# A fused attention and MLP kernel: the order of a key, two openings, one product and one mask on VectorE and ScalarE

## The chip, the cores and the metric

The kernel runs on one core of one Trainium2 chip. A core has five engines that run side by side, each through its own instructions in the order in which they were written: TensorE (PE in the profile; its weight loads, PEld, are listed apart), VectorE (DVE), ScalarE (ACT), GpSimd (POOL) and SyncE (SP). They wait for each other on semaphores. SP, ACT and POOL also issue DMAs. The metric is the time of one execution in device microseconds, as the median of several runs. All times below are microseconds.

## What is computed

Two stages follow each other. The first is a decaying linear attention over 4 batches, 8 heads, 768 positions and 64 channels, in blocks of 64 positions; the second is an MLP with a Mish activation over the 3072 tokens that come out.

```python
for b in range(nb):                      # attention, block after block
    intra = einsum('bhic,bhjc->bhij', qb, kb) * Dmask     # lam ** (i - j), i >= j
    intra = einsum('bhij,bhjd->bhid', intra, vb)
    inter = einsum('bhid,bhde->bhie', qb * lam_pow, kv_state)
    out[:, :, sl] = intra + inter
    kv_state = lam_block * kv_state + einsum('bhsd,bhse->bhde', kb * rev_pow, vb)
x = out.transpose(0, 2, 1, 3).reshape(3072, 512)
h = x @ w_in                                              # 512 -> 2048
g = h * tanh(log(1 + exp(h)))                             # Mish
out = g @ w_out                                           # 2048 -> 512
```

## The kernel before

**Tiling.** The kernel uses blocks of 128 positions, so there are 6 groups n = 0 to 5, each with one block of all 4 batches: 512 tokens. Block i = 4n + b is that of group n and batch b. While the MLP of group n runs, the attention of group n + 1 runs between its products, and the loads of group n + 2 are issued. The order on every engine is the order of the Python calls: nothing reorders it.

**The MLP as Strassen-like products.** In groups 1 to 5 both matrix products are made from quarters with seven instead of eight products, called P1 to P7. For the first MLP product the 16 blocks of hidden units are split into four sets of four: set 0 is called A, set 1 B, set 2 C; in groups 2 to 4 the fourth set is made by plain products, `duo(g, half)`: eight 128x256 products into a PSUM bank of the pair "ph", then a Mish on ScalarE (line 463). `set_unit(n, g, step)` (line 535) makes one step of a set: P1 to P7 are four products each at line 599. Around them stand

- `open` (line 576): a ScalarE copy of u1, which P1 left in SBUF, into the PSUM bank of z. P6, P7 and P4 then add to z.
- P5 leaves p5 (called p in the trace; for C in groups 2 to 4 by VectorE into "side", line 609, otherwise by ScalarE, line 611), and `mid` adds p5 to z on VectorE into y (line 561). P7 adds p5 to z into a buffer (hs or side, line 561), and its Mish is `m7`; `late` is the Mish of y; P4 ends with a Mish of z (line 557).
- `x_sum` (line 523): four token sums of x on VectorE, which P5, P6, P7 and P3 read.

The z of A lies in the only bank of "pS", that of B in the only bank of "pk". The score products of the pair at unit 2 use pS for their first tile, pk for their second and the two banks of "po" for the other two. So A's opening waits until the first mask has read its scores, and B's until the second has.

The second MLP product is `fast_unit(n, step, blk)`: eight 128x256 products a call at line 657. Its token sums `token_sum(n, i, part)` run on VectorE (line 640): gsum(i) has two halves, part 0 and 1, and P5, P6, P7 and P3 read gsum 0, 1, 2 and 3. In group 1 the z of this product lies in pk and is opened by a ScalarE copy (line 700) which is put off: it runs inside the next pair of scores, from the list `between`.

**The attention between them.** `scale_k(i)` is the key: one VectorE instruction that scales block i's k with its decay (ktil, line 265). `turn(i)` makes the key if it is not there yet and issues two DMA transposes from SP, of q and of the key (qraw and kraw, line 275). `pair_a` multiplies key and v of two blocks (pv, line 329) and adds the old state in four VectorE instructions (raw, line 289). `pair_s` makes the scores of two blocks (pS, line 352) and the state's part of the output (pO, line 360), then four VectorE masks (sb, line 368); whatever is in `between` runs after the first mask. `pair_o` adds masks times v to pO (line 381) and scales the result (xtok, line 389), which SP transposes into the x of the next group (xt, line 393).

**The order.** For each group a list `units` holds the MLP's steps, and dictionaries say what else is called behind unit u: `sums` (token sums), `ks` (keys), `turns`, `visit` (the pairs), `slots` (loads on POOL, each behind a small POOL copy, line 407, that waits for the latest Mish). Behind a unit the calls come in this order: loads, token sums, keys, turns, the pair, and at last x_sum. In groups 2 to 4, `pair_a` of the group's own blocks 2 and 3 stands at unit 0; `pair_s` of the next group's blocks 0 and 1 at unit 2 and its `pair_o` at unit 13; `pair_s` of the next group's blocks 2 and 3 at unit 17 and its `pair_o` at unit 21. The keys of the change are those of these last two blocks, so their transposes are read at unit 17. x_sum stands behind unit 2. Groups 1 and 5 have lists of their own.

Of the kernel before, what the change touches and what calls it, by code (L numbers as in the profile page):

```python
# [20 lines left out]
def kernel(  # L21
# [11 lines left out]
    B, H, S, D = q.shape  # L33
# [305 lines left out]
    between = []  # L339
# [285 lines left out]
    def token_sum(n, i, part):  # L625

        if (n, i) not in gsum:
            gsum[n, i] = work.tile([128, HK, 2 * C], F16, name=f"gsum{i}", tag=f"gsum{i}", bufs=1)
        w = HK // 2
        ks = slice(part * w, part * w + w)  # L630
        kh = slice(HK + part * w, HK + part * w + w)
        h = hsg[n]
        lo, hi = slice(0, 2 * C), slice(2 * C, 4 * C)
        a, b, op = (
            lambda: (h[:, ks, hi], h[:, kh, hi], ALU.add),
            lambda: (gsum[n, 0][:, ks, :], h[:, ks, lo], ALU.subtract),
            lambda: (h[:, ks, lo], h[:, ks, hi], ALU.subtract),
            lambda: (h[:, kh, lo], gsum[n, 1][:, ks, :], ALU.subtract),
        )[i]()
        nc.vector.tensor_tensor(out=gsum[n, i][:, ks, :], in0=a, in1=b, op=op)  # L640
# [191 lines left out]
    sums = {3: ((2, 0),), 7: ((2, 1),), 11: ((0, 0), (1, 0), (3, 0)), 15: ((0, 1), (1, 1)), 21: ((3, 1),)}  # L832
# [36 lines left out]
    for n in range(1, NG):  # L869
        r, s, t = Pair(), Pair(), Pair()  # L870
        r.n, r.bs, s.n, s.bs, t.n, t.bs = n, (2, 3), n + 1, (0, 1), n + 1, (2, 3)
        def duo(g, half):
            return mm1_duo, (n, g, half * (GT // 2), (half + 1) * (GT // 2))

        def part(g, *steps):
            return [(set_unit, (n, g, step)) for step in steps]

        later = []
        if n < NG - 2:
            later += [lambda f=f, i=(n + 2) * B + b + c: f(i)  # L880
                      for b in (0, 2) for f in (load_k, load_q) for c in range(2)]
        if 1 < n < NG - 1:
            for at, b in zip((2, 3, 6, 7), range(B)):
                later.insert(at, lambda i=(n + 1) * B + b: load_v(i))
        if n == 1:
            units = [[duo(0, 0)], [duo(1, 0)], [duo(2, 0)], part(0, "P1") + part(1, "P1") + [duo(3, 0)],
                     part(0, "P2") + part(1, "P2") + [duo(0, 1)]]
            units += [part(0, "open") + [duo(1, 1)], part(1, "open") + [(mm1_duo, (n, 2, GT // 2, GT, True))],
                      part(0, "P5") + [(duo_mish, (n, 2, 1))] + part(1, "P5"), part(0, "P6", "mid") + part(1, "P6"),
                      [duo(3, 1)] + part(1, "mid"), part(0, "P7") + part(1, "P7"), part(0, "P3") + part(1, "P3"),  # L890
                      part(0, "P4") + part(1, "P4") + part(0, "late") + part(1, "late")]
        else:
            units = [part(2, "P1") + part(0, "P1") + part(1, "P1"), part(2, "P2") + part(0, "P2") + part(1, "P2"),
                     [duo(2, 0)], [duo(3, 0)], part(0, "open") + [duo(2, 1)], [duo(3, 1)],
                     part(0, "P5") + part(2, "P5", "open"), part(0, "P6", "mid") + part(1, "open", "P5"),
                     part(2, "P6", "mid") + part(1, "P6", "mid"), part(0, "P3", "late", "P7"),
                     part(2, "P3", "late") + part(0, "m7") + part(2, "P7"),
                     part(1, "P3") + part(2, "m7") + part(1, "P7", "m7"),
                     part(2, "P4") + part(0, "P4") + part(1, "P4", "late")]
        sums = {12: ((0, 0), (0, 1), (1, 0), (1, 1)), 15: ((2, 0), (2, 1)), 18: ((3, 0),), 19: ((3, 1),)}  # L900
        visit = {}
        if n == 1:
            sums[9], sums[15], sums[19] = ((2, 0),), ((2, 1),), ((3, 0), (3, 1))
            sums[12] = (0, 0), (0, 1), (1, 0)
            del sums[18]
            visit = {10: (pair_a, s), 14: (pair_s, s), 18: (pair_o, s), 21: (pair_s, t), 24: (pair_o, t)}
            ks = {1: 9, 2: 10, 5: 11, 19: 12, 22: 13}
            turns = {1: 9, 5: 10, 7: 11, 19: 12, 22: 13}
            slots = range(6, 14)
        else:  # L910
            if n < NG - 1:
                visit = {0: (pair_a, r), 2: (pair_s, s), 13: (pair_o, s), 17: (pair_s, t), 21: (pair_o, t)}
            if n < NG - 2:
                visit[24] = pair_a, s
            ks = {1: (n + 1) * B + 2, 2: (n + 1) * B + 3, 11: (n + 2) * B, 11.5: (n + 2) * B + 1}
            turns = dict(zip((5, 6, 14, 15), ks.values()))
            slots = (1, 2, 3, 4, 5, 6, 7, 8, 9, 10, 12, 13)
        if n == NG - 1:
            K, L, A, B_ = 2, 3, 0, 1
            units = [part(K, "P1") + part(L, "P1") + part(A, "P1") + part(B_, "P1"),  # L920
                     part(K, "P2") + part(L, "P2") + part(A, "P2") + part(B_, "P2"),
                     part(K, "P5") + part(L, "P5") + part(A, "P5") + part(B_, "P5"),
                     part(K, "P6", "mid") + part(L, "P6", "mid") + part(A, "P6", "mid") + part(B_, "P6", "mid"),
                     part(K, "P3", "late") + part(L, "P3", "late") + part(K, "P7") + part(L, "P7"),
                     part(A, "P3", "late") + part(B_, "P3", "late") + part(A, "P7") + part(B_, "P7"),
                     part(K, "P4") + part(L, "P4") + part(A, "P4") + part(B_, "P4")]
            sums = {8: ((0, 0), (0, 1), (1, 0), (1, 1)), 10: ((2, 0), (2, 1)), 13: ((3, 0), (3, 1))}
        steps = ("P1", "P5", "P6", "P2", "P7", "P3", "P4")
        if n == NG - 1:
            steps = ("P1", "P2", "P5", "P6", "P7", "P3", "P4")  # L930
        units += [[(fast_unit, (n, step, blk))] for step in steps for blk in range(2)]
        for u, calls in enumerate(units):
            for fn, args in calls:
                fn(*args, **({"then": opened} if n == 1 and args[1:] == ("P1", 1) else {}))
            if n == 1 and u == 0:
                turn(8)
                look_s(7)
            if n == 1 and u == 2:
                f = look_kv(7)
                look_o(7)  # L940
                f()
                next_state(1, 1)
            for _ in range({0: 1, 1: 1, 2: 2, 3: 2}.get(u, 0) if n == 1 else 0):
                pace()
                ahead.pop(0)()
            if later and u in slots:
                pace()
                later.pop(0)()
            for i, part in sums.get(u, ()):
                token_sum(n, i, part)  # L950
            if 1 < n < NG - 1 and u == 11:
                next_state(n, 1)
            if n == NG - 2 and u in (22, 24):
                if u == 22:
                    more_sums()
                for i in range(2):
                    in_sum(3, u - 22 + i)
            for at in (u, u + 0.5):
                if ks.get(at, NG * B) < NG * B:
                    scale_k(ks[at])  # L960
            if turns.get(u, NG * B) < NG * B:
                turn(turns[u])
            if n == 1 and u == 7:
                for i in range(4):
                    in_sum(2, i)
            if u in visit:
                f, s_ = visit[u]
                s_.spare = ("pO", "pq") if n == 1 else ("po", "po") if u < 13 else ("pS", "pk")
                s_.scores = [(g, 2 if g in ("po", "ph") else 1) for g in (
                    ("pk", "pS", "ph", "ph") if n == 1 and u < 15 else ("pS", "ph", "po", "po") if n == 1 else  # L970
                    ("pS", "pk", "po", "po") if u < 13 else ("pS", "pk", "ph", "ph"))]
                if n == 1 and u == 14:
                    between += [opened.pop(), lambda: token_sum(1, 1, 1)]
                f(s_)
            if n == 1 and u == 10:
                next_state(2, 0)
            if u == (26 if n == 1 else 25):
                while owed:
                    owed.pop(0)()
            if u == (3 if n == 1 else 2 if n < NG - 1 else 0):  # L980
                for i in range(0, 4):
                    x_sum(n, i)
# [30 lines left out]
```

## Time and profile before

| | us |
|---|---|
| median of 3 runs | 197.01 |
| lowest and highest run | 196.90, 197.21 |
| the profiled execution | 196.51 |
| its span, first to last instruction | 194.7 |
| TensorE busy | 186.6 |
| VectorE busy | 166.4 |
| ScalarE busy | 104.0 |
| GpSimd busy | 80.9 |

The granted TensorE clock is 1.00 over the span. Group 1 is worked on from about 50 to 80 us, groups 2, 3 and 4 from 80.4, 109.4 and 138.3, group 5 from 167 on.

How to read the rows: a row of the timeline has the start, the length from the first start to the last end, the engine, the line, the operation, out<-in, the shape and the count of the instructions that it merges. A bracket tells how long the engine was idle before the row, and what ended that. The ends of matmuls are modelled, the starts are not; consecutive instructions of an engine overlap a little, so the step from one start to the next is shorter than an instruction. "issue" as the end of a wait means that the profile shows no single cause. A row of the waits has the total, the number and the longest. A row of the chain has start, length, engine, tile and line.

### The profile page before, as it was taken

What the parts mean: (1) busy time and instruction counts of PE and PEld (TensorE: products, weight loads), DVE (VectorE), ACT (ScalarE), POOL (GpSimd) and SP (SyncE); (2) the same over time, 40 slices, a digit from 0 to 9 for tenths busy, and PEclk for the clock granted to TensorE, in tenths of its full rate; (3) what the DMA queues carried; (4) which work ended last, traced back from release to release, by engine and by line L of the source; (5) the groups of instructions that cost most, each with busy time, mean ns of one, the idle gap of its engine ahead of it and who ended that gap; (6) DMA issues with size and microseconds to landing.
All of it is one profiled execution on the core that took longest, in us unless ns stands there. A gap on an engine that the chain in (4) does not pass through costs nothing.

```text
span 194.7 us, 5075 instructions
## 1 busy us (share of the span) xinstructions
PE 186.6 (96%) x2021; PEld 154.6 (79%) x2021; DVE 166.4 (85%) x325; ACT 104.0 (53%) x192; POOL 80.9 (42%) x129
## 2 busy tenths in 40 slices
PE   7888999899999999999999999999999999999993
PEld 3554447788888888988889988889988889888882
DVE  7889689699997999799999799998899799555893
ACT  5794674242687631477831477831578821688300
POOL 7997333489397850049730069630063000000000
PEclk9999999999999999999999999999999999999999
DMA  8999999999999998469999889999599023600014
GB/s 131 142 151 191 207 205 205 159 167 202 214 112 160 167 139 138 83 166 159 148 136 176 131 207 159 155 117 161 109 205 152 5 54 84 189 3 0 14 43 162
DMA packets 112458, 26.82 MB, mean 138 GB/s; under 512 B 101554, under 2 KB 112434, under 8 KB 112434
## 3 DMA queue, kind: packets, MB, share of 16 engines
q0 software_dynamic: 77552, 13.37, 95.9%
q1 hardware_dynamic: 31664, 10.76, 30.7%
q10 hardware_dynamic: 3218, 2.36, 4.0%
q8 instruction: 16, 0.26, 0.5%
q14 instruction: 8, 0.07, 0.2%
HBM read 27.26 MB, written 6.29 MB: 172 GB/s over the span
## 4 chain that ended last, share of the span: by engine, by line
PE 65%; DVE 13%; DMA 10%; POOL 8%; issue 2%; ACT 1%; POOLq 0%; DVEq 0%; ACTq 0%
PE z L657 13%; DMA wout<-in_moe_w_out_dram 10%; PE sz L599 9%; PE x L657 7%; PE y L657 5%; PE sx L599 5%; PE ph L451 4%; PE w L657 4%; DVE sb L368 3%; PE sw L599 3%; PE sy L599 3%; DVE raw L289 2%; PE pO L381 2%; POOL win L93 2%; POOL vz L78 2%
## 5 line engine op out<-in xcount | busy, mean ns | idle before, releaser
L657 PEld LDWEIGHTS <-gsum 128*128 128x128 f16 x384 | 36.6, 98 | 5.6 <-issue 1.1
L407 POOL COPY paced<-hsg 1x1 f16<-1x1 f16 x42 | 12.0, 285 | 48.3 <-ACT hsg L557 44.6
L657 PEld LDWEIGHTS <-hsg 128*128 128x128 f16 x272 | 26.1, 98 | 3.2
L75 POOL DMA_DIRECT2D qn<-in_q_dram x23 | 20.4, 886 | 7.0 <-DMA wout<-in_moe_w_out_dram 4.3
L657 PE MATMUL z<-tsum,gsum 128*128 128x256 f16 x176 | 22.5, 273 | 0.7 <-DVE tsum L483 0.6
L67 POOL DMA_DIRECT2D kn<-in_k_dram x23 | 20.5, 893 | 6.4 <-DMA win<-in_moe_w_in_dram 2.3
L78 POOL DMA_DIRECT2D vz<-in_v_dram x24 | 21.1, 884 | 4.0 <-DMA wout<-in_moe_w_out_dram 1.7
L657 PE MATMUL x<-wout,hsg 128*128 128x256 f16 x176 | 21.7, 273 | 0.0
L368 DVE TENSOR_TENSOR sb<-pS,maskT 128x512 f16<-128x512 f32 x32 | 20.0, 684 | 0.3 <-PE pS L352 0.2
L640 DVE TENSOR_TENSOR gsum<-hsg 128x1024 f16<-128x1024 f16 x24 | 15.7, 687 | 5.0 <-ACT hsg L557 3.4
L451 PE MATMUL ph<-xt,win 128*128 128x256 f16 x160 | 19.3, 273 | 0.0
L599 PEld LDWEIGHTS <-win 128*128 128x128 f16 x180 | 17.4, 98 | 1.9
L599 PEld LDWEIGHTS <-isum 128*128 128x128 f16 x160 | 15.6, 97 | 2.8 <-issue 0.8
L451 PEld LDWEIGHTS <-win 128*128 128x128 f16 x160 | 15.3, 98 | 2.0
L463 ACT ACTIVATE hsg<-ph 128x512 f16<-128x512 f32 x20 | 11.9, 595 | 6.4 <-PE ph L451 5.7
L416 PE MATMUL ph<-xt,win 128*128 128x512 f16 x64 | 14.5, 379 | 0.3 <-ACT xt L257 0.3
L265 DVE TENSOR_TENSOR ktil<-kn,lk 128x512 f16<-128x512 f16 (+1 forms) x22 | 14.5, 687 | 0.1
L599 PE MATMUL sx<-xt,win 128*128 128x256 f16 x120 | 14.6, 273 | 0.0
L719 ACT ACTIVATE osum<-z 128x512 f32<-128x512 f32 x4 | 2.4, 597 | 22.2 <-PE z L657 22.2
L561 DVE TENSOR_TENSOR sy<-sz,p 128x512 f32<-128x512 f32 x12 | 8.0, 693 | 5.6 <-PE sz L599 5.4
L428 ACT ACTIVATE hsg<-ph 128x512 f16<-128x512 f32 x16 | 9.6, 597 | 5.8 <-PE ph L416 5.8
L289 DVE TENSOR_TENSOR raw<-pv,state 64x256 f32<-64x256 f32 x24 | 10.1, 420 | 2.8 <-PE pv L329 2.4
(141 smaller groups left out, 378.0 us busy)
## 6 DMA issues: line engine op xcount, KB each, us to landing
out_dram<-osum SPq DMA_DIRECT2D x15, 256.0 KB, 2.7
vz<-in_v_dram POOLq DMA_DIRECT2D x24, 128.0 KB, 5.6
kn<-in_k_dram POOLq DMA_DIRECT2D x23, 128.0 KB, 5.6
qn<-in_q_dram POOLq DMA_DIRECT2D x23, 128.0 KB, 6.0
wout<-in_moe_w_out_dram POOLq DMA_DIRECT2D x4, 512.0 KB, 16.5
out_dram<-osum ACTq DMA_DIRECT2D x8, 256.0 KB, 3.2
win<-in_moe_w_in_dram POOLq DMA_DIRECT2D x3, 512.0 KB, 10.1
win<-in_moe_w_in_dram POOLq DMA_DIRECT2D x2, 256.0 KB, 6.2
```

The lines of the kernel that those rows point to most:

```text
L67: nc.gpsimd.dma_start(out=kn[i], in_=chunk_rows(k, i))
L75: nc.gpsimd.dma_start(out=qn[i], in_=chunk_rows(q, i))
L78: nc.gpsimd.dma_start(out=vz[i % NVB][:, :, 0:D], in_=chunk_rows(v, i))
L265: (nc.gpsimd if B + 1 < i < 2 * B else nc.vector).tensor_tensor(out=t, in0=kn[i], in1=bc(lk, 2, D), op=ALU.mult)
L289: nc.vector.tensor_tensor(out=raw[rs, b % 2, j0 : j0 + nj, :], in0=pv[rs, :, rs], in1=olds(rs), op=ALU.add)
L368: nc.vector.tensor_tensor(out=s.sb[m][t], in0=sc[m][t], in1=bc(maskT, 1, JP), op=ALU.mult)
L407: nc.gpsimd.tensor_copy(paced, mark[-1])
L416: nc.tensor.matmul(ph_t[ni][:, lo:hi], w_in(ni, kc), xt[n][:, kc, lo:hi], start=(kc == 0), stop=(kc == NKC - 1),)
L451: nc.tensor.matmul(t[:, m, lo - half * h : hi - half * h], w_in(ni, kc), xt[n][:, kc, lo:hi], start=(m == 0 and kc == 0), stop=(kc == NKC ...
L599: nc.tensor.matmul(t[:, m, :], lhs(kk, m), rhs(kk), start=(step in ("P1", "P5") and m == 0 and kk == 0), stop=(kk == KH - 1), skip_group_c ...
L640: nc.vector.tensor_tensor(out=gsum[n, i][:, ks, :], in0=a, in1=b, op=op)
L657: nc.tensor.matmul(places(n, key)[:, blk, lo:hi], lhs(kk, blk), rhs(kk, lo, hi), start=(fresh and kk == 0 and blk == 0), stop=(kk == HK - ...
```

## The change

Five edits of the order; no instruction is added, removed or changed.

- In groups 2 to 4 the keys that stood behind units 1 and 2 (both before the masks of unit 2, both after the raw rows of unit 0) now stand behind units 0 and 1; the one behind unit 0 comes ahead of the raw rows of the pair there. The `turns` read the same values in the same order and stay at units 5, 6, 14 and 15. `ks` had its entries at 1 and 2 by name: its first at unit 1, its second at unit 2.
- A's opening moves from unit 4 to unit 3, ahead of that unit's plain products and Mish.
- B's opening moves from unit 7, between A's P6 and B's P5, to unit 4, ahead of that unit's plain products and Mish.
- In unit 12 A's P4 comes first, then C's, then B's; it was C, A, B.
- In group 1 the first half of gsum(1) leaves unit 12, where it came ahead of the masks of unit 14, and goes into `between`, behind the first of these masks and the put-off opening, ahead of the second half.

```diff
-                     [duo(2, 0)], [duo(3, 0)], part(0, "open") + [duo(2, 1)], [duo(3, 1)],
-                     part(0, "P5") + part(2, "P5", "open"), part(0, "P6", "mid") + part(1, "open", "P5"),
+                     [duo(2, 0)], part(0, "open") + [duo(3, 0)], part(1, "open") + [duo(2, 1)], [duo(3, 1)],
+                     part(0, "P5") + part(2, "P5", "open"), part(0, "P6", "mid") + part(1, "P5"),
...
-                     part(2, "P4") + part(0, "P4") + part(1, "P4", "late")]
+                     part(0, "P4") + part(2, "P4") + part(1, "P4", "late")]
...
-            sums[12] = (0, 0), (0, 1), (1, 0)
+            sums[12] = (0, 0), (0, 1)
...
-            ks = {1: (n + 1) * B + 2, 2: (n + 1) * B + 3, 11: (n + 2) * B, 11.5: (n + 2) * B + 1}
+            ks = {0: (n + 1) * B + 2, 1: (n + 1) * B + 3, 11: (n + 2) * B, 11.5: (n + 2) * B + 1}
...
-                    between += [opened.pop(), lambda: token_sum(1, 1, 1)]
+                    between += [opened.pop()] + [lambda p=p: token_sum(1, 1, p) for p in range(2)]
```

## The prediction

> **What bounds the kernel now.** First the page, its engine table and its chain of work.
>
> ```profile
> PE 186.6 (96%) x2021; PEld 154.6 (79%) x2021; DVE 166.4 (85%) x325; ACT 104.0 (53%) x192; POOL 80.9 (42%) x129
> ...
> PE 65%; DVE 13%; DMA 10%; POOL 8%; issue 2%; ACT 1%; POOLq 0%; DVEq 0%; ACTq 0%
> ```
>
> TensorE is busy for 96% of the span and carries 65% of the chain. No part of the change adds or removes an instruction, so it can win only what TensorE idles, and lose only by new idle time. The weight loads show that idle time, since their ends are not modelled. Second view: the waits of the weight loads from 55 to 180 us.
>
> ```profile
> PEld L352 <- issue: 1.7, 8, 0.2
> PEld L599 <- issue: 0.8, 3, 0.3
> PEld L657 <- issue: 0.3, 1, 0.3
> ```
>
> The eight gaps ahead of line 352 are alike (0.21 each) and lie at the first score product of every pair; nothing in the change touches them. The other four are the prize: three at line 599, one per group 2, 3 and 4, and one at line 657 in group 1. Third view, the chain in order of time, at the start of group 3: what ends the wait at line 599.
>
> ```profile
> 114.83 1.88 DVE sb L368 x3
> 116.71 0.34 DVE xsum L523
> 117.09 1.03 PE sw L599 x8
> ```
>
> VectorE ends it: masks (sb), then the first token sum of x (xsum), then P5 of A (sw).
>
> **The change part by part.** *Group 1, the mask ahead of a token sum.* The timeline of all engines:
>
> ```profile
> 66.54 1.29 DVE L640 TENSOR_TENSOR gsum<-hsg 128x1024 f16<-128x1024 f16 x2
> ...
> 67.75 0.68 DVE L640 TENSOR_TENSOR gsum<-gsum,hsg 128x1024 f16<-128x1024 f16 x1
> 67.85 1.75 PEld L657 LDWEIGHTS <-gsum 128*128 128x128 f16 x17
> ...
> 68.46 0.69 DVE L368 TENSOR_TENSOR sb<-pS,maskT 128x512 f16<-128x512 f32 x1
> 69.07 0.68 DVE L640 TENSOR_TENSOR gsum<-gsum,hsg 128x1024 f16<-128x1024 f16 x1
> 69.25 0.58 ACT L700 ACTIVATE z<-x 128x512 f32<-128x512 f32 x1 [2.20 <-DVE sb L368]
> ...
> 69.67 1.88 DVE L368 TENSOR_TENSOR sb<-pS,maskT 128x512 f16<-128x512 f32 x3
> ...
> 69.88 1.62 PEld L657 LDWEIGHTS <-gsum 128*128 128x128 f16 x15 [0.28 <-issue]
> ```
>
> P6 (from 69.88) waits 0.28 for ScalarE's copy z, and that waits for the first mask at 68.46. The change moves the token sum of 67.75 behind this mask. The mask then starts at the end of the two sums (66.54 + 1.29 = 67.83, and 0.03 as between 68.43 and 68.46), 67.86; the copy follows 0.79 later as now (69.25 - 68.46), 68.65, and ends at 69.23. P5's sixteen products end at 69.60, so the wait goes whole, with 0.37 to spare. What is late next? The moved sum runs 68.46 to 69.14, ahead of P6; the other sum keeps 69.07 to 69.75, and P6 needs it from its fifth product, 69.60 + 4 x 0.109 = 70.04. The three later masks stay at 69.67 to 71.55; the products that read the last one (pO, after P6) would want it 0.28 earlier, at 71.68. All fit. Gain 0.28.
>
> *Groups 2 to 4, one key at unit 0.* In group 3, engine by engine:
>
> ```profile
> 111.12 1.74 DVE L289 TENSOR_TENSOR raw<-pv,state 64x256 f32<-64x256 f32 x4 [0.66 <-PE pv L329]
> 112.90 1.29 DVE L265 TENSOR_TENSOR ktil<-kn,lk 128x512 f16<-128x512 f16 x2
> 114.22 2.48 DVE L368 TENSOR_TENSOR sb<-pS,maskT 128x512 f16<-128x512 f32 x4
> 116.62 0.42 DVE L523 TENSOR_TENSOR xsum<-xt 128x512 f16<-128x512 f16 x1
> ```
>
> ```profile
> 113.42 0.65 PE L352 MATMUL pS<-qraw,kraw 64*128 64x128 f16 x16
> ...
> 114.23 2.79 PE L451 MATMUL ph<-xt,win 128*128 128x256 f16 x24
> ```
>
> ```profile
> 117.09 0.31 PEld L599 LDWEIGHTS <-isum 128*128 128x128 f16 x3 [0.24 <-issue]
> ...
> 118.73 0.45 PEld L599 LDWEIGHTS <-w 128*128 128x128 f16 x4
> 119.19 0.51 PEld L599 LDWEIGHTS <-isum 128*128 128x128 f16 x4
> ...
> 121.89 0.42 PEld L599 LDWEIGHTS <-isum 128*128 128x128 f16 x4
> 122.33 0.49 PEld L599 LDWEIGHTS <-w 128*128 128x128 f16 x4
> ```
>
> Between the state rows and the masks stand two keys (1.29), now both behind the raw rows. One of them goes ahead of the raw rows, into VectorE's wait for their products: 0.66 here. VectorE's waits for these products, summed:
>
> ```profile
> DVE raw L289 <- PE pv L329: 2.4, 3, 1.1
> ```
>
> So 1.1 in one group (group 2) and 0.66 in the two others. A key takes the engine for about 0.60 (1.29 for two, the second ending 0.69 after its start), so the wait hides it; without that cover it would cost its 0.60 again. The remaining key then ends at 112.90 + 0.69 = 113.59. The mask cannot start before its scores: its own eight of the sixteen products of 113.42 are through halfway, near 113.83; all sixteen end at 114.07. I take 113.86, since the first mask of this pair reads the first eight, and keep 114.07 as the worse end. Masks and x sum move up by 0.36 (at worst 0.15): xsum from 116.62 to 116.26, and with the 0.47 that P5 now starts behind it (117.09 - 116.62), P5 could start at 116.73. TensorE is through with its 24 products at 114.23 + 24 x 0.109 = 116.85. The 0.24 goes whole, 0.12 to spare. No DMA is moved: the transposes of these keys keep their units, and the loads that SP and POOL issue keep their order.
>
> *The openings of A and B.* Each is a ScalarE copy of u1 into z. ScalarE in group 3:
>
> ```profile
> 115.32 0.60 ACT L463 ACTIVATE hsg<-ph 128x512 f16<-128x512 f32 x1 [1.20 <-PE ph L451]
> ...
> 116.33 1.33 ACT L463 ACTIVATE hsg<-ph 128x512 f16<-128x512 f32 x2
> 117.72 0.60 ACT L611 ACTIVATE p<-sw 128x512 f32<-128x512 f32 x1
> 118.22 0.60 ACT L576 ACTIVATE sz<-side 128x512 f32<-128x512 f32 x1
> 118.74 0.59 ACT L576 ACTIVATE sz<-u 128x512 f32<-128x512 f32 x1
> ```
>
> B's opening (118.74) ends at 119.33, and B's P6 starts late: four loads take 0.51 where the others take 0.42 to 0.43, a loss of 0.08. Moved to unit 4 it takes the place that A's has now, between the Mish of 115.32 and that of 116.33. A's moves ahead of the Mish of 115.32, into a wait of 1.20. It has to wait for the first mask, whose bank it fills, and all later Mish stand behind it: mask at 113.86, opening at 114.65 (the 0.79 of above), next instruction 0.52 later (118.22 to 118.74), 115.17, ahead of 115.32. It is hidden; with the mask at 114.07 the Mish would begin 0.06 late. What is late next is ScalarE itself. The second Mish of the row at 116.33 starts at 117.06 (it ends at 117.66) and waits for TensorE, which does not move there; A's copy p can start 0.49 behind it, 117.55, though P5 is 0.24 earlier. Then C's opening starts at 118.05, ends at 118.65, and C's P6 starts near 118.69 rather than at the 118.61 that TensorE could. So 0.06 more is lost there than now (0.45 against 0.43 at 118.73).
>
> *P4 of A first.* C's P4 loses 0.07 now (0.49 against 0.42 at 122.33), since it waits for VectorE's sum.
>
> ```profile
> 121.76 0.69 DVE L561 TENSOR_TENSOR side<-sz,side 128x512 f32<-128x512 f32 x1 [0.18 <-PE sz L599]
> 122.64 0.69 DVE L561 TENSOR_TENSOR hs<-sz,p 128x512 f32<-128x512 f32 x1 [0.18 <-PE sz L599]
> ```
>
> The first row is C's sum, the second B's. With A first, C's P4 is ready in time; B's is still third. B's sum ends 1.33 after B's P7 begins (122.64 + 0.69 - 122.00, the load of 121.89 being 0.11 ahead) and needs some 0.05 to be seen; three steps of 0.436 take 1.31. The same 0.07 is then lost at B's P4. Gain 0.
>
> Per group: 0.24 (0.28 in group 2) + 0.08 - 0.06 = 0.26, 0.26 and 0.30.
>
> **A debit: the last key's transpose in group 2.** From the timeline, the tile's own answer and the view of the DMA queues:
>
> ```profile
> 91.14 1.31 SPq L275 DMA_TRANSPOSE kraw<-ktil  x1
> ...
> 99.81 0.62 PE L352 MATMUL pS<-qraw,kraw 64*128 64x128 f16 x16
> ```
>
> ```profile
> DMA to landing us min/median/max: 8.4/8.4/8.4
> ```
>
> ```profile
> q0 software_dynamic: 77552, 13.37, 95.9%
> ...
> kraw<-ktil SPq DMA_TRANSPOSE x16, 4.9
> ```
>
> It lands at 99.54; the second eight products of 99.81 need it, 0.22 on, at 100.03. With TensorE 0.58 earlier (0.28 + 0.30) they want it at 99.45: 0.09 and about 0.04 to be seen, a loss of 0.13, if the transfers do not move. Bounds: 0, if loads that start earlier also end earlier; the worse end is the second rival.
>
> **Sum.** 0.28 + 0.30 + 0.26 + 0.26 - 0.13 = 0.97. Group 5 starts behind TensorE and follows. The profiled execution took 196.51 (span 194.7 and 1.8 around it), 0.50 under the median 197.01; 195.54 on its own scale is 196.04 on that of the median.
>
> **The rivals.** *One: the early key gains nothing,* because the raw rows only move back behind it. The masks stay at 114.22, A's opening ends its hold at 115.53, the Mish of 115.32 slips by 0.21 and the last products with it, but the x sum is awaited until 117.09 anyway: only about 0.06 per group is left, 0.28 + 0.18 = 0.46, so 196.55. For it: only 0.06 between the wait of 0.66 and the key's 0.60. Against it: even 0.1 lost there still leaves VectorE ahead of the scores.
>
> *Two, slower: the transposes of group 2 land later.* POOL's loads are paced by ScalarE's Mish, so they too start 0.3 to 0.5 earlier. One more load ahead of the transpose costs up to 1.8 of all DMA engines: the load queue was busy 0.959 x 194.7 = 187 us for 13.37 MB, 128 KB are 0.98% of that. The landing would be 101.4, TensorE would stand for 1.95 rather than 0.13, and the time is 197.01 - 1.10 + 1.95 = 197.86. It decides from a landing at 100.9 (a loss of 1.49, 0.2% over the median). For it: 8.4 to landing here against a median of 4.9. Against it: an earlier load is also out of the way earlier. The Trainium skill's page "DMA: Bandwidth & Descriptors" (Queues, rings and completion order) states that each DMA engine takes turns between the queues that have work, packet by packet; by that rule it is this rival's direction if an added load is still in flight, and no run here shows yet how much.
>
> *Three: every wait named goes and none takes its place* (0.28 + 0.28 + 0.24 + 0.24 + 3 x 0.08 + 3 x 0.07 = 1.49): 195.52.
>
> **How the numbers follow.** A measurement of this kernel can tell about 0.2%, 0.39 us, from no change. Forecast (195.7 to 196.4): 0.62. Rival one: 0.14, just on the faster side of that bound, so half of it counts as same. Rival three: 0.06. Rival two: 0.08. The rest, 0.10, is waits I don't see and drift of the level: 0.07 faster, 0.03 same. Faster 0.82, same 0.10, slower 0.08. The range 195.5 to 196.7 takes in rivals one and three and leaves out rival two.
>
> **What would show it.** Right: no wait over 0.1 left at line 599's P5 in groups 2 to 4 nor at line 657's P6 in group 1; the first mask 0.43 behind the first score product; a key alone ahead of the raw rows, these at most 0.05 later against TensorE; 0.07 still lost at B's P4, and about 0.08 at C's P6. Wrong: a weight load that waits at line 352 in group 2's second pair by more than 0.3, a Mish held behind A's opening, or raw rows pushed back.

## The result and the profile after

The changed kernel takes 195.76 us (median of 22 runs, 194.97 to 197.15), the kernel before 197.05 (22 runs, 196.20 to 199.50). The ratio is 0.9943, with an interval of 0.9923 to 0.9962: 0.4 to 0.8% faster. It is taken over fast runs alone, without the two slow ones of the kernel before (199.22 and 199.50), so it is not the quotient of the two medians. The forecast was 196.0, in a range of 195.5 to 196.7. The profiled execution after took 195.52 (span 193.8), against 196.51 (span 194.7): 0.99 less, where the sum said 0.97.

First the engine table and the chain of work on the page of the kernel after.

```profile
PE 186.0 (96%) x2021; PEld 154.8 (80%) x2021; DVE 166.0 (86%) x325; ACT 104.4 (54%) x192; POOL 79.9 (41%) x129
...
PE 77%; DMA 13%; POOL 5%; DVE 2%; issue 1%; POOLq 0%
```

TensorE's share stays at 96% of a shorter span. Its busy time rests on modelled ends, so what it idles is not read from this row. VectorE's part of the chain has fallen from 13% to 2%, and TensorE's has risen from 65% to 77%. The waits of the weight loads, from 55 to 180 us, show the idle time itself, in one row:

```profile
PEld L352 <- issue: 1.7, 8, 0.2
```

The four waits at lines 599 and 657 are gone. The eight gaps at line 352 are the same as before.

Where the time went is read most exactly from the starts of TensorE's products, since starts are not modelled. The rows below are from the timeline of TensorE, kernel after: three of the eight first score products of a pair, and the first product of the last stage (fin).

```profile
67.16 0.62 PE L352 MATMUL pS<-qraw,kraw 64*128 64x128 f16 x16
...
99.35 0.62 PE L352 MATMUL pS<-qraw,kraw 64*128 64x128 f16 x16
112.95 0.65 PE L352 MATMUL pS<-qraw,kraw 64*128 64x128 f16 x16
...
188.53 1.93 PE L770 MATMUL fin<-tsum,hsg 128*128 128x256 f16 x24
```

All nine start at 67.16, 74.64, 84.30, 99.35, 112.95, 128.02, 141.63, 156.70 and 188.53; in the kernel before at 67.06, 74.81, 84.47, 99.81, 113.42, 128.74, 142.35, 157.67 and 189.50. The stretches between them:

| stretch | before | after | difference | forecast |
|---|---|---|---|---|
| group 1's mask and P6 (67 to 75) | 7.75 | 7.48 | -0.27 | -0.28 |
| to group 2's first pair | 9.66 | 9.66 | 0 | 0 |
| group 2's first MLP product | 15.34 | 15.05 | -0.29 | -0.30 |
| group 2's second (debit of the transpose) | 13.61 | 13.60 | -0.01 | +0.13 |
| group 3's first MLP product | 15.32 | 15.07 | -0.25 | -0.26 |
| group 3's second | 13.61 | 13.61 | 0 | 0 |
| group 4's first MLP product | 15.32 | 15.07 | -0.25 | -0.26 |
| the rest, to fin | 31.83 | 31.83 | 0 | 0 |
| from the first row to the last | 122.44 | 121.37 | -1.07 | -0.97 |

What lies ahead of the first row took 0.10 longer in this execution. It varies from 66.65 to 68.87 over the profiles of all kernels below, where the order ahead of it is the same. So the stretch from the first row to the last is what I compare kernels by; it is called **the stretch** from here on.

### The profile page after: what moved, and what is told of

Same layout as the page of the kernel before. It is cut to its first block, busy times and chain, and to the rows that moved or that the text cites. A ratio compares the mean times of both kernels' runs of the same rounds, so it can differ in the third digit from the quotient of the medians.

```text
span 193.8 us, 5078 instructions
## 1 busy us (share of the span) xinstructions
PE 186.0 (96%) x2021; PEld 154.8 (80%) x2021; DVE 166.0 (86%) x325; ACT 104.4 (54%) x192; POOL 79.9 (41%) x129
## 4 chain that ended last, share of the span: by engine, by line
PE 77%; DMA 13%; POOL 5%; DVE 2%; issue 1%; POOLq 0%
PE z L657 13%; PE sz L599 10%; DMA wout<-in_moe_w_out_dram 10%; PE ph L451 9%; PE x L657 8%; PE sx L599 7%; PE y L657 5%; PE w L657 5%; DMA win<-in_moe_w_in_dram 3%; PE sw L599 3%; PE sy L599 3%; PE pS L352 2%; PE pO L381 2%; POOL vz L78 2%; POOL kn L67 1%; PE pv L329 1%
## 5 line engine op out<-in xcount | busy, mean ns | idle before, releaser
L407 POOL COPY paced<-hsg 1x1 f16<-1x1 f16 x42 | 10.9, 260 | 47.0 <-ACT hsg L557 43.7
L599 PEld LDWEIGHTS <-win 128*128 128x128 f16 x180 | 17.4, 98 | 1.9
L451 PEld LDWEIGHTS <-win 128*128 128x128 f16 x160 | 15.3, 98 | 2.0
L416 PEld LDWEIGHTS <-win 128*128 128x128 f16 x64 | 6.0, 97 | 7.4 <-DMA win<-in_moe_w_in_dram 0.8
```

The source lines that it names most:

```text
L407: nc.gpsimd.tensor_copy(paced, mark[-1])
L416: nc.tensor.matmul(ph_t[ni][:, lo:hi], w_in(ni, kc), xt[n][:, kc, lo:hi], start=(kc == 0), stop=(kc == NKC - 1),)
L451: nc.tensor.matmul(t[:, m, lo - half * h : hi - half * h], w_in(ni, kc), xt[n][:, kc, lo:hi], start=(m == 0 and kc == 0), stop=(kc == NKC ...
L599: nc.tensor.matmul(t[:, m, :], lhs(kk, m), rhs(kk), start=(step in ("P1", "P5") and m == 0 and kk == 0), stop=(kk == KH - 1), skip_group_c ...
```

## The experiments

Each run changes the order alone and leaves no work out; one also swaps the engines of two copies. Where a run has one execution (one time and one profile), what is said rests on its trace: single times vary by more than these parts are worth (194.97 to 197.15 for the changed kernel). The first four make one part of the change alone, on the kernel before.

**The keys alone.**

```diff
-            ks = {1: (n + 1) * B + 2, 2: (n + 1) * B + 3, 11: (n + 2) * B, 11.5: (n + 2) * B + 1}
+            ks = {0: (n + 1) * B + 2, 1: (n + 1) * B + 3, 11: (n + 2) * B, 11.5: (n + 2) * B + 1}
```

> Only the keys move (units 0 and 1 in groups 2 to 4). Theory: the first mask starts 0.43 behind the first score product, P5 of A no longer waits (0.28 + 0.24 + 0.24 gone), but ScalarE's copy p behind the last Mish and B's late opening take part of it back: C's P6 waits about 0.06, B's P6 still about 0.08. Net 0.22 + 0.18 + 0.18 = 0.58 off the span between the first pair of group 2 and the first product of group 5. Group 1's wait of 0.28 at line 657 stays. Rival (the key only pushes the raw rows back): P5 waits as before and nothing is won.

One execution took 196.93. The stretch is 122.32, which is only 0.12 less than before. But the waits of the weight loads, from 55 to 180 us, show what stands against the gain:

```profile
PEld L352 <- issue: 1.7, 8, 0.2
PEld L381 <- issue: 0.4, 1, 0.4
PEld L657 <- issue: 0.3, 1, 0.3
```

The three waits of P5 at line 599 are gone, and that at line 657 (the other part of the change) is still there. A new one of 0.4 stands at line 381, the product of masks and v; the step between two of its products is 0.445 too long. Without it the stretch would be 121.88, or -0.56; 0.58 was expected. The wait at line 381 is none of my theories; later runs are about it. In the timeline of the weight loads of this run, C's P6 and B's P6 lose what they were to lose (0.06 and 0.08 over 0.42):

```profile
119.29 0.48 PEld L599 LDWEIGHTS <-w 128*128 128x128 f16 x4
119.79 0.50 PEld L599 LDWEIGHTS <-isum 128*128 128x128 f16 x4
```

**The openings alone.**

```diff
-                     [duo(2, 0)], [duo(3, 0)], part(0, "open") + [duo(2, 1)], [duo(3, 1)],
-                     part(0, "P5") + part(2, "P5", "open"), part(0, "P6", "mid") + part(1, "open", "P5"),
+                     [duo(2, 0)], part(0, "open") + [duo(3, 0)], part(1, "open") + [duo(2, 1)], [duo(3, 1)],
+                     part(0, "P5") + part(2, "P5", "open"), part(0, "P6", "mid") + part(1, "P5"),
```

> Only the openings of A and B move. Theory: without the early key the first mask stays where it was, A's opening waits for it and holds the Mish of the third plain product by about 0.2; the last plain products (line 451) wait 0.19 and P5 then only 0.05, so P5 starts where it did; B's P6 loses its 0.08, C's P6 gains about 0.02 to 0.04 of wait. Net about 0.06 per group, 0.18 in all. Rival: the held Mish costs its 0.2 per group on top of P5's wait, 0.4 slower in all.

One execution took 196.76; the stretch is 122.48, with 0.26 of it at line 381 again, so -0.22 without that (-0.18 was expected). Here the mechanism of rival one can be seen, since the masks are still late: ScalarE and then the weight loads in group 3.

```profile
115.39 0.60 ACT L576 ACTIVATE sz<-u 128x512 f32<-128x512 f32 x1 [0.89 <-DVE sb L368]
115.92 0.58 ACT L463 ACTIVATE hsg<-ph 128x512 f16<-128x512 f32 x1
```

```profile
116.56 0.75 PEld L451 LDWEIGHTS <-win 128*128 128x128 f16 x7 [0.20 <-issue]
117.32 0.47 PEld L599 LDWEIGHTS <-isum 128*128 128x128 f16 x4
```

A's opening waits for the first mask, the Mish stands behind it, and the plain products at line 451 wait 0.20 for the bank that the Mish frees. P5 then loses only 0.05 (0.47 against 0.42) where it lost 0.24. The hold costs nothing net while P5 waits for VectorE anyway; that was rival one's reasoning.

**P4 of A first, alone.**

```diff
-                     part(2, "P4") + part(0, "P4") + part(1, "P4", "late")]
+                     part(0, "P4") + part(2, "P4") + part(1, "P4", "late")]
```

> Only P4 of A goes first in unit 12. Theory: the wait of 0.07 goes from C's P4 to B's P4 in each group, net 0. Rival: it goes whole, 0.21 won over three groups.

One execution took 196.69; the stretch is 122.61, of which 0.17 is at line 381: a gain of 0.00 (its time is the lowest of these four all the same). The weight loads of C's and B's P4 in group 3:

```profile
122.76 0.42 PEld L599 LDWEIGHTS <-w 128*128 128x128 f16 x4
123.19 0.49 PEld L599 LDWEIGHTS <-isum 128*128 128x128 f16 x4
```

C's no longer waits, and the 0.07 has moved to B's.

**The mask of group 1 alone.**

```diff
-            sums[12] = (0, 0), (0, 1), (1, 0)
+            sums[12] = (0, 0), (0, 1)
...
-                    between += [opened.pop(), lambda: token_sum(1, 1, 1)]
+                    between += [opened.pop()] + [lambda p=p: token_sum(1, 1, p) for p in range(2)]
```

> Only group 1's first mask goes ahead of the token sum. Theory: the wait of 0.28 at line 657 goes whole, with about 0.37 to spare, and nothing takes its place in group 1: 0.27 off from there on. The other waits at line 599 stay at 0.28, 0.24, 0.24. Rival: the token sum, now behind the mask, or the later masks make P6 or the products behind it wait, and less than 0.15 is left.

One execution took 197.11; the stretch is 122.18, or -0.26 (-0.27 was expected). Its waits of the weight loads keep the three at line 599 (0.8 in all) and have none at line 657.

The four parts give -0.56, -0.22, 0.00 and -0.26 without the waits at line 381: -1.04 together, against -1.07 for the whole change. So they add up, and the keys are the largest.

**The whole change without its P4 part.**

```diff
-                     part(0, "P4") + part(2, "P4") + part(1, "P4", "late")]
+                     part(2, "P4") + part(0, "P4") + part(1, "P4", "late")]
```

> The changed kernel with P4 of C first again. Theory: the wait of 0.07 is back at C's P4 and gone at B's, the span is that of the changed kernel within 0.05. Rival: 0.2 slower over three groups.

One execution took 196.36. The stretch is 122.28, with 0.90 of it at line 381. Without that it is 121.38, the same as after: P4's order is worth nothing in the company of the other parts either. The 0.90 is the largest case of the new wait, and here the profile names its releaser. First TensorE in group 3, then the load itself and its landing:

```profile
123.88 0.28 PE L381 MATMUL pO<-vz,sb 128*128 128x64 f16 x4
124.90 0.51 PE L381 MATMUL pO<-vz,sb 128*128 128x64 f16 x12 [0.74 <-DMA vz<-in_v_dram]
```

```profile
117.22 0.88 POOL L78 DMA_DIRECT2D vz<-in_v_dram  x1
...
DMA to landing us min/median/max: 7.6/7.6/7.6
```

The fifth of the sixteen products is the first that reads the second block's v. That block was issued at 117.22 and took 7.6 to land, at 124.8; the product wanted it at about 124.0.

**Two loads called earlier in group 2.** This was to set the forecast's debit against rival two: if loads that start earlier push back the transpose of the last key, two more loads ahead of it should push it far.

```diff
+            if n == 2 and u == 1:
+                later.pop(0)()
+                later.pop(0)()
```

> The changed kernel with two more of group 2's loads issued at unit 1, so that two more loads are ahead of the transposes of the last key. If the transposes land later by what a load takes of the DMA engines (1.8 each), the last one lands near 103 and TensorE waits some 3 at line 352 in group 2's second pair. If earlier loads are out of the way earlier, it lands within 0.5 of 99.3 and nothing waits.

One execution took 196.08; the stretch is 121.74, of which 0.36 is at line 381, so 121.38 without it. The transpose of the last key in this run, and its landing; then the loads of POOL around its issue:

```profile
90.73 1.34 SPq L275 DMA_TRANSPOSE kraw<-ktil  x1
...
DMA to landing us min/median/max: 7.7/7.7/7.7
```

```profile
89.81 0.87 POOL L75 DMA_DIRECT2D qn<-in_q_dram  x1
...
90.79 0.87 POOL L78 DMA_DIRECT2D vz<-in_v_dram  x1
```

It lands at 98.4, not later but 1.1 earlier than in the kernel before (91.14 + 8.4), and the scores at 99.5 do not wait for it. But this run does not decide on rival two. The load of 89.81 is the group's sixth, and the seventh was issued 0.06 behind the transpose. So six loads were ahead of it, as many as in the kernel before and the changed one, and those behind the first two were 0.6 earlier than in the changed one. No run here puts one load more ahead of this transpose. Nor can the earlier landing be put down to the edit: the changed kernel itself had 8.5 to landing in one profile and 7.5 in another (the next run). What is shown of rival two is that its delay did not come: the loads of the changed kernel started 0.2 to 0.5 earlier than before, as it said, and in none of the profiles does line 352 wait longer than in the kernel before. The wait at line 381 is that of group 3, whose loads this edit does not touch. In group 2 the second v load was issued 0.60 earlier than in the changed kernel (87.76 against 88.36), and landed no earlier: it took 7.6 instead of 6.7.

**The changed kernel again,** beside the two runs above, on their chip.

> The changed kernel itself, beside the next one. Theory: 0.5% under the kernel before (0.9943 as measured), weight loads wait only at line 352; C's P6 waits 0.06 and B's P4 0.07 in groups 2 to 4.

The median is 196.38 against 197.16 there; the ratio is 0.9959 (0.9933 to 0.9985). The stretch is 121.57, with 0.19 at line 381, so 121.38 without it, as in the two runs above. The wait at line 381 is 0 in one profile of this kernel and 0.19 in another: it changes between executions of one program.

**Two of the leftovers removed at once.** B's P7 goes ahead of its P3, so that B's P4 finds its sum ready. A's copy p is made by VectorE and C's by ScalarE, behind C's opening, so that C's opening need not stand behind A's copy on ScalarE.

```diff
-                     part(0, "P5") + part(2, "P5", "open"), part(0, "P6", "mid") + part(1, "P5"),
+                     part(0, "P5") + part(2, "P5"), part(0, "P6", "mid") + part(1, "P5"),
...
-                     part(1, "P3") + part(2, "m7") + part(1, "P7", "m7"),
+                     part(1, "P7") + part(2, "m7") + part(1, "P3", "m7"),
...
-            if 1 < n < NG - 1 and g == 2:
+            if 1 < n < NG - 1 and g == 0:
...
+                if 1 < n < NG - 1 and g == 2:
+                    nc.scalar.activation(place("z"), first[n, g, "u1"], AF.Copy)
```

> The changed kernel with its two left-over waits attacked: VectorE copies A's p5 and ScalarE C's, with C's opening ahead of that copy (so the copy of p no longer stands between the last Mish and C's opening), and B's P7 comes ahead of B's P3, so that B's sum is 0.44 earlier against B's P4. Theory: both waits (0.06 and 0.07, in three groups) go, 0.39 less on the span than the changed kernel, 0.2%. Rival: VectorE, which has nearly no slack there, makes A's P3 or C's P3 wait instead and it is no faster.

The median is 196.39, the ratio 0.9968 (0.9936 to 1.0000). By the time it can't be told from the changed kernel (196.38 on the same chip), but the stretch is 121.78: 0.41 worse than after. VectorE and then the weight loads of this run in group 3 show the turn:

```profile
117.70 0.42 DVE L523 TENSOR_TENSOR xsum<-xt,xsum 128x512 f16<-128x512 f16 x1
118.04 0.68 DVE L609 COPY p<-sw 128x512 f32<-128x512 f32 x1
```

```profile
117.95 0.54 PEld L599 LDWEIGHTS <-isum 128*128 128x128 f16 x5
118.78 0.31 PEld L599 LDWEIGHTS <-isum 128*128 128x128 f16 x3 [0.29 <-issue]
```

The last of A's P5 has started by 117.5, but its copy stands on VectorE behind the four token sums of x, until 118.72. B's P5, which needs that bank, waits 0.29 to 0.32 for it in each group. So the 0.06 at C's P6 was bought with a wait five times as long. By the trace this edit failed; the other half of it is tried alone below.

**The v loads of the next group's first pair ahead of its k loads** in POOL's queue, on the changed kernel. It was made to end the wait at line 381.

```diff
-            for at, b in zip((2, 3, 6, 7), range(B)):
+            for at, b in zip((0, 1, 6, 7), range(B)):
```

> The changed kernel with the v loads of the next group's blocks 0 and 1 first among the loads of groups 2 and 3 (they were third and fourth). Theory: the waits at line 381 that some runs of these kernels show (0.19 in one run of the changed kernel, 0.36, 0.45 and 0.90 in others) are the second of these loads landing late; issued about 2.5 earlier it lands 2.5 to 3 ahead of its products, no wait at line 381 is left in any run, and the median is 0.1 to 0.4 under that of the changed kernel. Rival: the waits move to another load (k or q, now two places later) or the DMA engines, not the order, set the landing, and line 381 still waits.

The median is 197.93 against 197.31 for the kernel before on that chip: 1.0034 (0.9999 to 1.0069), so the gain is gone. The new row among the waits of the weight loads in this run, and then one of VectorE's in group 3:

```profile
PEld L657 <- DVE gsum L640: 1.9, 4, 1.1
```

```profile
125.52 0.69 DVE L265 TENSOR_TENSOR ktil<-kn,lk 128x512 f16<-128x512 f16 x1 [1.09 <-DMA kn<-in_k_dram]
126.13 1.28 DVE L640 TENSOR_TENSOR gsum<-hsg 128x1024 f16<-128x1024 f16 x2
```

Line 381 waits no more: the second v load is now issued at 86.04 in group 2 and lands at 92.5. Now the k load of a key comes late, the key holds VectorE for 1.09, and the token sums behind it hold P5 of the second MLP product. The steps between these products put the cost at 1.51 (0.40 in group 2, 1.11 in group 3); without it the stretch (122.88) is 121.37, the same as after. The queue's order decides which of the loads is late.

**The same with B's P7 ahead of its P3.**

```diff
-            for at, b in zip((2, 3, 6, 7), range(B)):
+            for at, b in zip((0, 1, 6, 7), range(B)):
...
-                     part(1, "P3") + part(2, "m7") + part(1, "P7", "m7"),
+                     part(1, "P7") + part(2, "m7") + part(1, "P3", "m7"),
```

> The kernel of the run before, with B's P7 ahead of B's P3 as well. Theory: the wait of 0.07 at B's P4 goes in groups 2 to 4 (VectorE's sum for it starts up to 0.44 earlier), C's P6 still waits 0.06; 0.21 under the run before in the trace, which timing alone can hardly tell. Rival: B's P3, now later, delays its Mish and with it the second product; the 0.07 comes back there.

The median is 197.97, 1.0030 (0.9992 to 1.0069). Its profiled execution took 200.81, far above that median, so I read only where it waited, not how long: at line 657 for gsum, and VectorE at the key for the k load, as in the run above. The wait at B's P4 is gone.

**The kernel before with the v loads first.**

```diff
-            for at, b in zip((2, 3, 6, 7), range(B)):
+            for at, b in zip((0, 1, 6, 7), range(B)):
```

> The kernel before, with only the v loads first as above. Theory: no wait at line 381; the waits at line 599 and 657 are as in the kernel before (0.28, 0.24, 0.24 and 0.28); same as before or up to 0.3 faster. Set beside the changed kernel with v first it gives what the change is worth without that wait: 1.06 by the trace. Rival: the v load is never late in the kernel before, and nothing changes.

The median is 197.36, 1.0005 (0.9969 to 1.0041): no difference that can be measured. The stretch is 122.61, with 0.16 in new waits for gsum. So this order of the loads brought nothing to either kernel. The expectation that the change is worth 1.06 with it failed: the changed kernel with this order has the longer stretch (122.88) and the higher median (197.93). Without its 1.51 of waits it would have its gain, so by the trace the change pays with this order only if the k loads land in time. That they cost more on the changed one fits its earlier products, but one profile of each can't show that, with the spread that these loads have.

**The changed kernel with B's P7 ahead of its P3,** and nothing else.

```diff
-                     part(1, "P3") + part(2, "m7") + part(1, "P7", "m7"),
+                     part(1, "P7") + part(2, "m7") + part(1, "P3", "m7"),
```

> The changed kernel with B's P7 ahead of B's P3 in groups 2 to 4, and nothing else. Theory: VectorE's sum for B's P4 starts up to 0.44 earlier, so the 0.07 at B's P4 goes in all three groups and nothing takes its place, since B's P3 is needed by no one before the second product; 0.21 under the changed kernel in the waits of the trace, 0.4 to 0.7% under the kernel before. A wait at line 381 for a v load may show or not, as in the changed kernel. Rival: B's P3, one step later, holds its Mish (late) and with it the copy that opens the second product's z; the wait comes back there.

The weight loads of A's, C's and B's P4 in group 3 (the last three rows):

```profile
122.09 0.42 PEld L599 LDWEIGHTS <-isum 128*128 128x128 f16 x4
122.53 0.43 PEld L599 LDWEIGHTS <-w 128*128 128x128 f16 x4
122.97 0.42 PEld L599 LDWEIGHTS <-isum 128*128 128x128 f16 x4
```

The 0.07 at B's P4 is gone, in all three groups. The stretch is 121.17, which is 0.20 under after and 1.27 under before. The times do not show it: the median is 196.30, against 196.72 for the kernel before on that chip, 0.9976 (0.9947 to 1.0005), where 0.4 to 0.7% was expected, and this interval does not even exclude the time of the kernel before. By the trace it is the best order of all those tried; by the times it is not proved better than after.

## Why the prediction was right, step by step

**What bounds the kernel.** Right. TensorE's idle time was the prize. By the starts of its products the four waits at lines 599 and 657 cost 1.00 and B's P6 0.25 in three groups; both are gone, 0.17 was lost anew at B's P5 and C's P6, and the stretch fell by 1.07.

**Group 1's mask.** Right: 0.27 for 0.28. The timeline after, all engines:

```profile
67.95 0.69 DVE L368 TENSOR_TENSOR sb<-pS,maskT 128x512 f16<-128x512 f32 x1
...
68.56 1.28 DVE L640 TENSOR_TENSOR gsum<-gsum,hsg 128x1024 f16<-128x1024 f16 x2
...
68.74 0.58 ACT L700 ACTIVATE z<-x 128x512 f32<-128x512 f32 x1 [1.59 <-DVE sb L368]
...
69.71 1.91 PE L657 MATMUL z<-tsum,gsum 128*128 128x256 f16 x16
```

The opening of z starts 0.79 behind the mask, as taken, and ends at 69.32, with 0.39 to spare against 69.71 (0.37 was said). Of the token sums, the moved half runs inside the cover that was named.

**The keys.** Right, and rival one fell with it. VectorE in group 3 after:

```profile
109.91 0.68 DVE L265 TENSOR_TENSOR ktil<-kn,lk 128x512 f16<-128x512 f16 x1
110.65 1.75 DVE L289 TENSOR_TENSOR raw<-pv,state 64x256 f32<-64x256 f32 x4
112.43 0.69 DVE L265 TENSOR_TENSOR ktil<-kn,lk 128x512 f16<-128x512 f16 x1
113.38 2.48 DVE L368 TENSOR_TENSOR sb<-pS,maskT 128x512 f16<-128x512 f32 x4 [0.27 <-PE pS L352]
```

The raw rows start at 110.65. Before, it was 111.12, and the scores have moved from 113.42 to 112.95, also by 0.47: against TensorE the raw rows were not pushed back at all. The early key took the wait of 0.66 and nothing more. The masks start 0.43 behind the first score product, which is the better of the two ends I gave (0.44 against 0.65), and VectorE itself idles 0.27 ahead of them.

**The openings.** Right in all three terms, though half of the loss lies one product earlier than it was looked for. The weight loads of group 3 after, from A's P5 to B's P6:

```profile
116.29 0.43 PEld L599 LDWEIGHTS <-isum 128*128 128x128 f16 x4
...
117.16 0.89 PEld L599 LDWEIGHTS <-isum 128*128 128x128 f16 x8
118.06 0.48 PEld L599 LDWEIGHTS <-w 128*128 128x128 f16 x4
118.55 0.42 PEld L599 LDWEIGHTS <-isum 128*128 128x128 f16 x4
```

P5 starts without a wait and B's P6 takes 0.42 where it took 0.51. C's P6 takes 0.48 where it took 0.45, so 0.03 more is lost there, not 0.06. The other 0.03 is lost just before it: A's P6 and B's P5 (the row of 117.16) take 0.89 where they took 0.86, since B's P5 needs the bank that A's copy p frees at 117.68. In sum it is the 0.06 of the forecast, and the late copy behind both is the one that was named. ScalarE after:

```profile
115.86 1.33 ACT L463 ACTIVATE hsg<-ph 128x512 f16<-128x512 f32 x2
117.09 0.59 ACT L611 ACTIVATE p<-sw 128x512 f32<-128x512 f32 x1
117.57 0.61 ACT L576 ACTIVATE sz<-side 128x512 f32<-128x512 f32 x1
```

A's copy follows the last Mish with no idle time between them, and C's opening follows the copy by 0.48. Rival three, in which no wait takes another's place, fell on this row and on P4.

**P4 of A first.** Right: nothing gained, the 0.07 is lost at B's P4 instead. The run without it has the same stretch.

**The debit.** This is the term that was mis-sized: 0.13 was taken, and 0 was measured (13.60 against 13.61). Its step said that the transfers do not move. The transpose did move. The last key's transpose after, and its landing:

```profile
90.83 1.38 SPq L275 DMA_TRANSPOSE kraw<-ktil  x1
...
DMA to landing us min/median/max: 8.5/8.5/8.5
```

SP issued it 0.31 earlier than before (91.14), and it landed at 99.3. The products that read it wanted it 0.22 behind 99.35, at 99.57. So the better of the prediction's two ends came true. But a sum from one landing could not have been exact: from issue to landing this transpose took 7.5 to 8.5 in the profiles here, and in the second profile of the changed kernel it landed 1.5 ahead of its use. That spread is larger than the 0.13. The Trainium skill's page "DMA: Bandwidth & Descriptors" (Queues, rings and completion order) was cited there for queues that take turns. These runs neither show nor exclude that rule; what it was held to make possible here, a later landing, did not come, and no run here adds a load ahead of the transpose.

**The sum.** -1.10 without the debit, -1.07 measured on the stretch. That the profiled executions differ by 0.99, so near to the 0.97 of the sum, is partly luck: the missing debit and the 0.10 longer front cancel. The difference of the medians, 1.29, is larger than the trace's, but the interval of the ratio (0.75 to 1.52, from 0.9962 and 0.9923) holds both, as does that of the repeat (0.30 to 1.32).

**What the prediction did not see.** It said of DMAs only that the loads keep their order and checked one transpose. It missed that the second v load of the next group's first pair lands on the very edge of its use. Before, and then after, in group 2:

```profile
88.55 0.87 POOL L78 DMA_DIRECT2D vz<-in_v_dram  x1
...
DMA to landing us min/median/max: 7.1/7.1/7.1
```

```profile
88.36 0.87 POOL L78 DMA_DIRECT2D vz<-in_v_dram  x1
...
95.29 0.63 PE L381 MATMUL pO<-vz,sb 128*128 128x64 f16 x16
```

Before, it landed at 95.66, and the fifth product wanted it at 95.88 (95.76 and 0.12 on). So 7.33 lay between issue and use; after, it is 95.41 - 88.36 = 7.05, and in group 3 it went from 6.99 to 6.78. The change takes 0.28 and 0.21 of that margin, since the products move up more than the load does. The v loads on that edge took 5.9 to 7.6 to land in these profiles, so the wait falls on some executions: of the ten profiles with part or all of the change and the loads in the old order, six had one, of 0.17 to 0.90, and the one profile of before had none. In all six the fifth product starts 0.04 to 0.05 behind the landing of this load. The keys' and openings' runs had it, but so did the run with P4 alone, whose loads lie as before. How much of it belongs to the change and how much to chance, these few profiles can't say, nor do the times: the intervals of the first measurement and the repeat overlap. What decides how long a load takes stays open: issued 0.6 earlier behind the same loads it landed no earlier in the one profile of that, and moved ahead of the k loads it landed in time and made those late.

## What to carry to other kernels

When the bound engine moves up by a few tenths, list every transfer that it reads in that stretch with its landing and its first use, not only the one that looks latest: this gain of 1 us lives beside loads with 0.2 us of margin. A short instruction that is moved into another engine's wait is free only if the wait is longer than it (0.66 against 0.60 here); check that what stood behind it keeps its start against the bound engine. And removing one wait of 0.06 is worth less than the queue that the moved work has to stand in (0.29 behind four token sums).

## What the runs showed of the hardware

The time from issue to landing of a load of the same size at the same place among the loads varies by 1.7 us over eleven profiles (5.9 to 7.6 for the second v load of group 3), more than the whole change is worth; two executions of one program, the changed kernel, had 5.9 and 6.9. In one profile the first two v loads of group 2 were issued 0.6 us earlier behind the same loads, took 7.3 and 7.6 instead of 6.7 and landed no earlier against their products. An instruction whose operands come from a load makes that spread a wait on its whole engine: one key that was 1.09 late on VectorE cost TensorE 1.05 at the next product that read VectorE's sums.
